# Moving SyncE's closing waits for loads and transposes ahead of the last five stores

## The chip, the cores and the metric

The kernel runs on one core of a Trainium2 chip. The metric is the device time of one execution in microseconds, as a median of several executions. The profile gives a second number, the span from the program's first to its last own instruction, which is about 1.7 us shorter than the time here.

SyncE is the engine that issues most of the transfers here; it computes nothing. A semaphore is a counter that a transfer raises when its data have arrived, and on which an engine can wait.

## The reference, cut to what matters

The program is one transformer layer on 2048 tokens of width 448: linear attention, then a gated feed-forward block. The change touches no arithmetic. Only the last line matters for it, because its result is what the last stores carry.

```python
x = A_x
h = x + _A_ref(_layernorm(x, axis=-1), A_wqkv, A_w_phi, A_wo)
h2 = h + _B_ref(_layernorm(h, axis=-1), B_w_gate, B_w_up, B_w_down)
return h2          # 1 x 2048 x 448, bf16: 16 tiles of 128 tokens
```

## The kernel before

The kernel is a list of operations with a fixed order for each engine. Every transfer gets a semaphore of its own: the rings are at least as long as the number of transfers of their kind (48 for loads, 64 for transposes, 17 for stores).

```python
if dma is not None and nring:
    lst = self.ring.setdefault(dma, [])
    ...
    o.sem = (dma, len(lst) % nring)
    o.val = 16 * (len(lst) // nring + 1)
```

The result tile is finished by VectorE and stored by SyncE. The last tile is finished and stored in two parts, of 320 and 128 columns. The bar in the last comment line marks the place to which the change moves the waits.

```python
def finish(t, b, lo=0, hi=D, nm=""):
    op("dve", "fin%d%s" % (t, nm), lambda e: e.scalar_tensor_tensor(
        out=h_sb[:, t, lo:hi], in0=bk(b)[:, lo:hi], scalar=0.5, in1=h_sb[:, t, lo:hi], op0=ALU.mult, op1=ALU.add),
       r=[B(b), ("x", t)], w=[("xo", t, lo)])
    op("sp", "out%d%s" % (t, nm), lambda e: e.dma_start(out_t[:, t, lo:hi], h_sb[:, t, lo:hi]), r=[("xo", t, lo)], dma="out", nring=17)

# end of SyncE's order:
#   ... out10 out7 out8 out9 out6 out11 | out13 out12 out14 out15 out15b
```

The engine's program is written out by `body`. SyncE ends with a wait for every semaphore that a transfer has ever raised.

```python
last_out = {}
for o in ops:
    if o.dma is not None:
        last_out[o.sem] = max(last_out.get(o.sem, 0), o.val)
...
def body(eng, q=queues[e], e=e):
    seen = {}
    for o in q:
        for j in o.waits:
            ...
            eng.wait_ge(sems[p.sem], p.val)
        ins = o.fn(eng)
        ...
    if e == "sp":
        for sem, v in last_out.items():
            eng.wait_ge(sems[sem], v)
```

The softmax here doesn't subtract the row's maximum and nothing guards it: scores larger than these inputs give would overflow.

## Time and profile before

| | before |
|---|---|
| time, median of 3 runs | 207.08 us (207.05 to 207.18) |
| span | 205.46 us |
| TensorE busy | 197.3 us, 96% |
| last addition on VectorE ends | 201.67 us |
| last store issued / landed | 201.70 / 203.19 us |
| first / last closing wait starts | 202.13 / 205.00 us |
| closing stretch: from the end of the last addition to the end of the span | 3.79 us |

SyncE's instructions are not counted as busy on the page, so the page alone shows an end in which nothing seems to happen. Its instructions are found by the lines of the source that they come from. After its waits it leaves the program by a branch, here put down to line L152 and called the closing branch below. The view of one source line gives, for each kind of instruction, the count, the shortest, median and longest duration in ns, and the start of the first and the last. For a store it also gives the time from issue to landing, which is the moment at which its semaphore is complete. Times to a hundredth of a microsecond for single waits and landings are the trace's own records. The prediction shows these lines.

### The profile page before, as it was taken

To read this page: it belongs to the slowest core of one execution; us is meant where nothing else is said; L and a number is where in the kernel's file an instruction comes from. 1 tells how busy PE (TensorE), PEld (TensorE's weight loads), DVE (VectorE), ACT (ScalarE), POOL (GpSimd) and SP (SyncE) were. 2 spreads that over 40 slices of the span, in tenths; PEclk is the share of its full clock that TensorE was granted. 3 is DMA by queue.
4 is the path that set the end of the run, shared out by engine and by line. 5 is a ranking of instruction groups with operands and counts; after the bars stand their busy time and mean duration, and the time that the engine had idled before them with its cause. 6 is when DMAs were issued, how large, how long until landed. Compare 5 with 4: busy or idle time off the path is not lost.

```text
span 205.5 us, 5834 instructions
## 1 busy us (share of the span) xinstructions
PE 197.3 (96%) x2474; PEld 113.2 (55%) x2474; DVE 135.7 (66%) x340; ACT 97.3 (47%) x195; POOL 57.9 (28%) x98
## 2 busy tenths in 40 slices
PE   7999999989979999999999999999999999999991
PEld 2945556655447877786445444444555555544451
DVE  4899999978899987777768877346332512371252
ACT  2899999889882543522333442334323112320220
POOL 4699998943344401300041020001400000000000
PEclk9999999999999999999999999999999999999999
DMA  6975352999622462130007411120311000012002
GB/s 163 302 138 121 56 102 58 288 260 342 169 51 54 77 76 50 32 79 0 3 0 87 114 29 26 24 54 24 78 48 26 3 0 3 0 58 79 0 11 78
DMA packets 32866, 16.25 MB, mean 79 GB/s; under 512 B 25096, under 2 KB 31944, under 8 KB 32840
## 3 DMA queue, kind: packets, MB, share of 16 engines
q1 hardware_dynamic: 32336, 15.86, 33.9%
q8 instruction: 19, 0.31, 0.6%
q10 hardware_dynamic: 504, 0.03, 0.2%
q14 instruction: 7, 0.06, 0.1%
HBM read 8.34 MB, written 1.84 MB: 50 GB/s over the span
## 4 chain that ended last, share of the span: by engine, by line
PE 91%; ACT 4%; DVE 2%; issue 0%
PE psum L291 81%; PE psum L847 5%; PE psum L473 3%; PE psum L487 1%; ACT eq L648 1%; ACT eq L647 1%; PE psum L562 1%; ACT Wk L480 1%; ACT junk L751 1%; ACT x_sb L743 1%; DVE kvz L678 1%; PE psum L549 1%; DVE b_sb L712 0%; DVE c_sb L715 0%; DVE oT L480 0%
## 5 line engine op out<-in xcount | busy, mean ns | idle before, releaser
L291 PE MATMUL psum<-xnT,wg_sb 64*128 64x512 bf16 (+1 forms) x490 | 93.4, 333 | 0.4 <-ACT eq L648 0.2
L291 PE MATMUL psum<-xnT,wu_sb 64*128 64x512 bf16 (+1 forms) x490 | 92.9, 333 | 0.0
L819 ACT ACTIVATE sg_sb<-psum 128x512 bf16<-128x512 f32 (+1 forms) x70 | 35.0, 512 | 89.4 <-PE psum L291 88.8
L820 DVE SCALAR_TENSOR_TENSOR hhT<-sg_sb,psum 128x512 bf16<-128x512 bf16 (+1 forms) x70 | 38.9, 576 | 52.6 <-ACT sg_sb L819 52.1
L291 PEld LDWEIGHTS psum<-xnT,wg_sb 64*128 64x128 bf16 x490 | 44.3, 94 | 22.8 <-DVE hhT L820 4.8
L291 PEld LDWEIGHTS psum<-xnT,wu_sb 64*128 64x128 bf16 x490 | 44.3, 94 | 12.8
L291 PE MATMUL psum<-wd_sb,hhT 64*128 64x448 bf16 x336 | 36.9, 349 | 0.0
L291 PEld LDWEIGHTS psum<-wd_sb,hhT 64*128 64x128 bf16 x336 | 17.6, 94 | 14.5 <-DVE x_sb L746 0.6
L617 POOL TENSOR_TENSOR phi<-hhT,rs 128x896 bf16<-128x896 bf16 x14 | 24.0, 1738 | 0.9 <-PE psum L291 0.4
L291 PE MATMUL psum<-Wk,xnT 64*128 64x448 bf16 x112 | 22.3, 350 | 0.3 <-ACT Wk L480 0.2
L291 PE MATMUL psum<-wv_sb,xnT 64*128 64x448 bf16 x112 | 22.4, 351 | 0.1
L754 POOL TENSOR_SCALAR ve<-ssq 128x1 f32<-128x1 f32 x16 | 3.1, 192 | 66.1 <-ACT junk L751 65.7
L613 DVE TENSOR_REDUCE ss<-hhT 128x32 f32<-128x896 bf16 x16 | 17.0, 1060 | 0.7 <-ACT hhT L610 0.7
L291 PE MATMUL psum<-xnT,Wq 64*120 64x512 bf16 x112 | 15.0, 385 | 0.1
L724 POOL TENSOR_TENSOR o_pad<-c_sb,rden 128x448 bf16<-128x448 bf16 x10 | 9.3, 937 | 15.6 <-DVE rden L720 13.4
L291 PE MATMUL psum<-wo_o,oT 64*128 64x448 bf16 x56 | 13.2, 350 | 0.0
L291 PE MATMUL psum<-wo_e,oT 64*128 64x448 bf16 x56 | 13.1, 349 | 0.0
L751 ACT ACTIVATE junk<-x_sb,nm 128x448 bf16<-128x448 bf16 x16 | 10.6, 662 | 2.0 <-DVE nm L749 2.0
L847 PE MATMUL psum<-wd_sb,hhT 128*128 128x448 bf16 (+2 forms) x70 | 11.1, 316 | 0.0
L854 DVE SCALAR_TENSOR_TENSOR x_sb<-psum,x_sb 128x448 bf16<-128x448 f32 (+2 forms) x17 | 9.4, 591 | 2.1 <-PE psum L847 1.6
L494 DVE BATCH_NORM_STATS2 st<-x_sb 128x6 f32<-128x448 bf16 x16 | 9.4, 608 | 2.0 <-DMA x_sb<-in_A_x_dram 2.0
L291 PEld LDWEIGHTS psum<-Wk,xnT 64*128 64x128 bf16 x112 | 7.6, 94 | 5.3 <-ACT hhT L610 0.7
(87 smaller groups left out, 243.0 us busy)
## 6 DMA issues: line engine op xcount, KB each, us to landing
out_dram<-x_sb SPq DMA_DIRECT2D x15, 112.0 KB, 1.8
x_sb<-in_A_x_dram SPq DMA_DIRECT2D x7, 224.0 KB, 4.7
wd_sb<-in_B_w_down_dram SPq DMA_DIRECT2D x7, 224.0 KB, 9.6
wg_sb<-in_B_w_gate_dram SPq DMA_DIRECT2D x3, 448.0 KB, 8.8
wu_sb<-in_B_w_up_dram SPq DMA_DIRECT2D x3, 448.0 KB, 6.7
wv_sb<-in_A_wqkv_dram SPq DMA_DIRECT2D x2, 224.0 KB, 5.2
wk_sb<-in_A_wqkv_dram SPq DMA_DIRECT2D x2, 196.0 KB, 3.2
wo_e<-in_A_wo_dram SPq DMA_DIRECT2D x1, 336.0 KB, 8.3
```

Of the source, the lines that this page charges most:

```text
L291: p = e.matmul(o, lhsT=w, rhs=r, start=st, stop=sp, tile_position=(row, 0))
L473: p = e.matmul(bk(3)[:, 0:size], lhsT=zero[:, 0:P], rhs=zero[:, 0:size], start=True, stop=True)
L494: op("dve", "bst%d" % t, lambda e: e.bn_stats(st1[:, t, :], x_sb[:, t, :]), r=[("x", t)], w=[("st1", t)])
L613: op("dve", "ss%d" % t, lambda e: e.tensor_reduce(ss[:, s, :], eks, AX.X, ALU.add), r=[("ek", s)], w=[("ss", s)])
L617: return e.tensor_tensor(phi[:, sp, :, :, :].rearrange("p b a n -> p (b a) n")[:, :, 0:56].rearrange("p b (h d) -> p b h d", h=2), eks.rea ...
L724: return e.tensor_tensor(o_pad[:, t % NO, off:off + D].rearrange("p (h d) -> p h d", h=H), c_sb[:, t % NS, :, 0:DH], rden[:, t % NS, :][:, ...
L751: op("act", "sq%d" % t, lambda e: e.activation(junk[:, t % 2, :], h_sb[:, t, :], ACT.Square, bias=nm2[:, t:t + 1], accum_out=ssq2[:, t:t + ...
L754: op("pool", "ve%d" % t, lambda e: e.tensor_scalar(ve2[:, t:t + 1], ssq2[:, t:t + 1], 1.0 / D, EPS, op0=ALU.mult, op1=ALU.add), r=[("ssq2" ...
L819: op("act", "sig" + nm, lambda e: e.activation(sg_sb[:, k, 0:N], bk(bg)[:, 0:N], ACT.Tanh, scale=0.5), r=[B(bg)], w=[("sg", k)])
L820: op("dve", "hh" + nm, lambda e: e.scalar_tensor_tensor(out=hhT[(t0 // 4) % NHH][:, ff, ns], in0=sg_sb[:, k, 0:N], scalar=1.0, in1=bk(bu)[ ...
L847: p = e.matmul(bk(b)[:, lo:hi], lhsT=hb[:, ff, TS(t)], rhs=wd_sb[:, ff, lo:hi], start=ff == 0, stop=ff == FT - 1)
L854: op("dve", "fin%d%s" % (t, nm), lambda e: e.scalar_tensor_tensor(out=h_sb[:, t, lo:hi], in0=bk(b)[:, lo:hi], scalar=0.5, in1=h_sb[:, t, l ...
```

## The change

The intent is to pay for the waits for loads and transposes, all long finished, at a point where SyncE is idle anyway, and to keep only the waits for stores at the end.

```diff
-                        for o in q:
+                        for n, o in enumerate(q):
+                            if e == "sp" and n == len(q) - 5:
+                                for sem, v in last_out.items():
+                                    if sem[0] != "out":
+                                        eng.wait_ge(sems[sem], v)
                             for j in o.waits:
...
                         if e == "sp":
                             for sem, v in last_out.items():
-                                eng.wait_ge(sems[sem], v)
+                                if sem[0] == "out":
+                                    eng.wait_ge(sems[sem], v)
```

## The prediction

> **What bounds the kernel now.** I read the page first, then the chain of waits in order of time for the last 26 us, then the timeline of the end, and last the sources of SyncE's own instructions there. The page's first part and its chain give the setting: TensorE works almost throughout, and no change on SyncE can shorten that part.
>
> ```profile
> span 205.5 us, 5834 instructions
> PE 197.3 (96%) x2474; PEld 113.2 (55%) x2474; DVE 135.7 (66%) x340; ACT 97.3 (47%) x195; POOL 57.9 (28%) x98
> ```
>
> The chain of waits, cut to its end, shows where the computing stops: the last matmuls of the down projection, then one VectorE addition that ends at 201.38 + 0.29 = 201.67 us. The span is 205.46 us (205.5 on the page), so 3.8 us follow in which no engine computes. The change can touch only these.
>
> ```profile
> 196.24 5.12 PE psum L847 x38
> 201.36 0.02 issue
> 201.38 0.29 DVE x_sb L854
> ```
>
> What fills the 3.8 us is all on SyncE. The timeline shows its last five stores, which start from 199.30 us and are issued by 199.30 + 2.78 = 202.08 us. The store line L857, cut to the last store, gives its time from issue to landing; it was issued at 201.70 us and so landed at about 201.70 + 1.5 = 203.2 us (the trace's semaphore records say 203.19). The wait line L174 has 48 instructions that follow the last store one after another, from 202.13 to 205.00 us. The same view, cut to what starts after 203.2 us, shows that 31 of the 48 still come then: they wait for nothing that has not happened.
>
> ```profile
> 199.30 2.78 SPq L857 DMA_DIRECT2D out_dram<-x_sb  x5
> ...
> DMA to landing us min/median/max: 1.5/1.5/1.5
> ...
> L174 SPq EVENT_SEMAPHORE  x48: 27/28/28, 202.1 to 205.0; - x48
> ...
> L174 SPq EVENT_SEMAPHORE  x31: 27/28/28, 203.2 to 205.0; - x31
> ```
>
> The table of stretches agrees: from 203.0 us nothing moves on the DMA engines, and no engine computes, yet the span goes on for 2.4 us.
>
> ```profile
> 203.00:203.20 0.20, 0.00 (x0) 0.00 (x0) 0.00 (x0) 0.00 (x0) 0.00 (x0) 1.00 0.00 0
> 203.20:205.50 2.30, 0.00 (x0) 0.00 (x0) 0.00 (x0) 0.00 (x0) 0.00 (x0) 0.89 0.00 0
> ```
>
> So the end is set by SyncE's sequencer walking through its list of waits. First come 1.1 us of the list under the stores' landing, then 1.8 us of it alone, and then the closing steps of the program, whose line L152 shows SyncE as the last to arrive (its branch at 205.06 us, where VectorE's drain began at 201.4 and the others' earlier).
>
> ```profile
> L152 DVEq DRAIN  x1: 330/330/330, 201.4 to 201.4; - x1
> L152 SPq COMPARE_BRANCH  x1: 41/41/41, 205.1 to 205.1; - x1
> ```
>
> **What the Trainium skill says.** "Perfetto Trace Analysis", the section on a sequencer-only instruction: the profile reports only the execution; decoding and the waiting itself lie outside. The trace agrees. A wait is shown with 28 ns, but the 48 start (205.00 - 202.13) / 47 = 0.061 us apart; I therefore price a wait by its spacing and not by its duration. "Advanced Engine Details and Errata", in Network/Comms, gives 50-100 ns for a sequencer's reading of a semaphore; 61 ns for an instruction that checks two is in that range. "Perfetto Trace Analysis", DMA Instruction - HWDGE: a DMA's profiled window ends when the sequencer is free, the data move later, and the last descriptor, which raises the semaphore, waits for confirmation of the write, which "can cause a surprisingly long delay especially when the write target is HBM". The trace has 0.38 us for the issue of the last store, against 1.5 us to its landing. "DMA: Bandwidth & Descriptors", Rules for kernel authors, advises issuing a DMA early and waiting late, so that its fixed cost overlaps; here the waits for old transfers are the work that can overlap.
>
> **The change, part by part.** *How many waits.* Every transfer has a semaphore of its own. The source has 32 loads from SyncE (9 of x, 4 of k and v, 4 of wo, 8 of gate and up, 7 of down), 4 small ones from ScalarE, 44 transposes (4 of q, 12 + 14 + 14 of activations) and 17 stores: 97 semaphores. The trace has 48 instructions of two waits each, and the 97th sits on the closing branch. Of the 97, 17 are for stores, so 80 move.
>
> *Where they go.* The last five entries of SyncE's list are out13, out12, out14, out15 and out15b, which are the five of the timeline from 199.30 us. The entry before them, out11, is issued by 185.67 us in the trace's records. The 80 waits thus land between 185.67 and 199.30 us, where SyncE now does nothing but wait 13.6 us for VectorE. All are for transfers long finished: the last transpose is issued at 153.07 us and lands 2.4 us later, the last load is issued at 70.0 us. They should pass without stopping, in 40 instructions x 0.061 = 2.4 us, over by about 188.2 us, 11 us before out13 can be issued. The wait of out13 for VectorE may be joined to the last of them instead of sitting on the store itself, which would make that store some 0.06 us later; the next store starts 0.6 us after this one's issue has ended and is bound by VectorE, so nothing is handed on.
>
> *What stays at the end.* 17 waits: by the same pairing 8 instructions and one on the branch. Were nothing late they would take 8 x 0.061 = 0.49 us and be done at 202.13 + 0.49 = 202.62 us. But now they meet the stores in flight. The last five land, by the trace's semaphore records, at 200.99, 201.91, 202.45, 202.84 and 203.19 us. The waits are paired outward from the middle of the list in the trace before, so the last pair should hold the last store: it passes 0.02 to 0.03 us after the landing (the spacing that the first VectorE statistics show after their loads), at about 203.21 us.
>
> *The tail.* From the start of the last wait instruction before (205.00 us) to the end of the span (205.46 us) are 0.47 us: branch, drain, exchange between engines. It is the same code after.
>
> *The sum.* The new end is 203.21 + 0.47 = 203.68 us in place of 205.46: 1.78 us less. Check by counting: 31 instructions after the landing, less the one that must remain, are 30 x 0.061 = 1.8 us. TensorE's 197 us, the loads, the order and number of all other instructions are unchanged, and so is what the measured time has beyond the span (207.08 - 205.46 = 1.6 us). 207.08 - 1.78 = **205.30 us**, a ratio of 0.991.
>
> **The rivals.** *Nothing is gained, the landing is the bound already.* Then the waits would be free beside the store's confirmation, and the time stays 207.1 us. For it: waits for something already past sound free, and each shows 28 ns. Against: 31 of them start after the landing, and the closing branch follows directly on the last.
>
> *All 40 instructions count.* This would give 40 x 0.061 = 2.4 us, so 204.6 us. Against: the 17 waits left would end at 202.62 us, before the last store has landed at 203.19; the landing takes the place of the list as the bound and keeps 0.6 us of it. Only if the landing itself came earlier could this happen, and nothing in the change makes it earlier.
>
> *The moved waits hold up the stores.* If one of the 80 were for something late, or if they were slower than the 13.6 us of idle time, the last five stores would start late and the end would move out, 1:1. To lose all of the gain, they would have to last 13.6 + 1.8 us, six times their price. Nothing in the profile supports it: the last of those transfers is over 30 us before.
>
> *The waits are dear only under the profiler.* If recording made each of them slower, the unprofiled end would already be closer to the landing. Against: the profiled run took 207.22 us, 0.14 us more than the median of the others. If all of that lay in the 48 waits, 3 ns each, the gain would fall by 30 x 0.003 = 0.1 us.
>
> **Range and chances.** The store's landing is the uncertain term: the 17 stores took 1.5 to 3.0 us, but the ones at the end, without other traffic, 1.5 to 1.8. A last store that needs 1.8 costs 0.3 us of the gain. Runs of the kernel before spread over 0.13 us. The profiler's rival takes off at most 0.1 us. On the other side I see only a landing 0.1 us earlier and the spread. So 205.0 to 205.7 us for 8 in 10. Within 2% is everything from 202.94 to 211.22 us. Faster by over 2% would need 4.1 us, more than the whole 3.8 us in which nothing computes; slower would need the stores held up by over 5 us. Chances: faster 0.01, same 0.98, slower 0.01.
>
> **What would show each step right or wrong.** (1) The wait line inside the loop shows some 40 instructions between about 185.7 and 188.2 us, spaced by 0.06; fewer or slower ones would break the count or the price. (2) The five last stores start at the same times as before, from 199.3 us; later ones would mean the third rival. (3) At the end stand 8 wait instructions, and the last passes at about 203.2 us, within 0.05 us of the last landing; one that passes at 202.6 would mean that the landing isn't waited for as I think. (4) The span is about 203.7 us and the timed difference 1.8 us like the profiled one; a timed difference clearly smaller than the profiled one would mean the profiler's rival. What would make me wrong overall is a landing of the last store at other than 1.5 us, or a part of the 1.6 us beyond the span that ran beside the list of waits and now has to be waited for.

## The result, and the profile after

The changed kernel took 205.43 us (median of 4 runs, 205.24 to 206.15), beside 207.06 us of the kernel before (4 runs, 207.00 to 207.18). The ratio is 0.9927, with a 95% interval of 0.9903 to 0.9951. Ratios here are the mean time of one kernel's runs over that of the other's of the same rounds, so they are not quite the ratio of the quoted medians. The gain of 1.63 us is below 2% and counts as the same.

The changed kernel's lines are five further down in the source: the stores are L862, the moved waits L165, the closing waits L179. First come its span and its TensorE time, from the page.

```profile
span 203.7 us, 5834 instructions
PE 196.7 (97%) x2474; PEld 111.6 (55%) x2474; DVE 135.9 (67%) x340; ACT 97.4 (48%) x195; POOL 57.9 (28%) x98
```

The number of instructions is unchanged, and the span is shorter by 1.75 us. The chain of waits, cut to its end, shows that the computing ends nearly where it did (201.41 + 0.29 = 201.70 us, 0.03 us later than before).

```profile
196.26 5.12 PE psum L852 x38
201.39 0.02 issue
201.41 0.29 DVE x_sb L859
```

SyncE's own lines show the rest. The fence gives, in this order, the moved waits, the last five stores in the timeline (start and length in us), the time from issue to landing of the very last store (issued at 201.73 us), the closing waits, those closing waits that start after 203.2 us, and the closing branch.

```profile
L165 SPq EVENT_SEMAPHORE  x39: 28/28/28, 185.8 to 188.1; - x39
...
199.40 2.71 SPq L862 DMA_DIRECT2D out_dram<-x_sb  x5
...
DMA to landing us min/median/max: 1.5/1.5/1.5
...
L179 SPq EVENT_SEMAPHORE  x8: 28/28/28, 202.2 to 203.2; - x8
...
L179 SPq EVENT_SEMAPHORE  x1: 28/28/28, 203.2 to 203.2; - x1
...
L152 SPq COMPARE_BRANCH  x1: 41/41/41, 203.3 to 203.3; - x1
```

The 39 moved instructions lie between 185.76 and 188.11 us, after which SyncE waits another 11.2 us for VectorE. At the end 8 instructions are left where there were 48, and one instead of 30 starts after the last landing. (The prediction said 31: a view cut to a window also counts an instruction that is under way at its start, and one had begun at 203.18 us.) The list of SyncE's waits, which had no wait for a store in the kernel before, now has one (columns: total, times, longest).

```profile
SPq L170 <- DVE x_sb L859: 11.2, 1, 11.2
SPq L179 <- DMA out_dram<-x_sb: 0.7, 2, 0.4
```

So the bound at the end has changed hands: before, it was the walk through the list; now it is the landing of the last store, at 203.22 us. The closing stretch fell from 3.79 to 2.01 us, by 1.78 us. What is left of it is 0.03 us to the issue of the last store, 1.49 us to its landing and 0.49 us from there to the end.

### The profile page after: what moved, and what is told of

It is laid out like the page before. It is cut to its first block, busy times and chain, and to the rows that moved or that the text cites. A ratio compares the mean times of both kernels' runs of the same rounds, so it can differ in the third digit from the quotient of the medians.

```text
span 203.7 us, 5834 instructions
## 1 busy us (share of the span) xinstructions
PE 196.7 (97%) x2474; PEld 111.6 (55%) x2474; DVE 135.9 (67%) x340; ACT 97.4 (48%) x195; POOL 57.9 (28%) x98
## 4 chain that ended last, share of the span: by engine, by line
PE 89%; DVE 4%; ACT 3%; DMA 1%; issue 1%; POOL 0%; DVEq 0%
PE psum L296 82%; PE psum L852 5%; DVE st L499 2%; DMA x_sb<-in_A_x_dram 1%; ACT eq L653 1%; ACT eq L652 1%; PE psum L567 1%; ACT junk L756 1%; ACT x_sb L748 1%; PE psum L492 1%; DVE kvz L683 1%; DVE mv L500 0%; DVE b_sb L717 0%; DVE c_sb L720 0%; POOL rst L512 0%
```

## The experiments

The theory is this. A wait for something that is already past costs SyncE about 0.061 us for each instruction, and an instruction holds two waits. No run tells whether the 0.061 us are the price of checking a semaphore or of any instruction of SyncE's. These instructions are free as long as they lie under another wait (the 13.6 us for VectorE, the 1.5 us for the last landing); beyond that, they move the end one for one. The main rival says that every instruction of the list counts, without a floor. Others say that only the number of waits at the very end matters, or that moving itself costs something.

Single runs of one kernel differ by a few tenths of a microsecond. In the kept traces with the same end (the changed kernel, a0, a1, a2, b4) the last addition ends anywhere from 201.47 to 201.82 us, but the closing stretch is 2.01 us in each, so it is the sharper measure. All numbers in one table; "waits after landing" counts the closing wait instructions that start later than the last store's landing. The a runs share one set of rounds and of runs of the kernel before, the b runs another, and the c runs a third, on another chip; the line of the kernel before shows its first three runs.

| kernel | closing wait instructions | waits after landing | closing stretch, us | time, us (median) | ratio to before (95% interval) |
|---|---|---|---|---|---|
| before | 48 | 30 | 3.79 | 207.08 | 1 |
| changed | 8 | 1 | 2.01 | 205.43 | 0.9927 (0.9903 to 0.9951) |
| a0 changed, again | 8 | 1 | 2.01 | 205.24 | 0.9892 (0.9863 to 0.9922) |
| a1 none moved | 8 | 1 | 2.01 | 205.32 | 0.9896 (0.9863 to 0.9929) |
| a2 16 kept at the end | 16 | 1 | 2.01 | 205.31 | 0.9897 (0.9867 to 0.9927) |
| a3 40 kept at the end | 28 | 10 | 2.57 | 206.05 | 0.9930 (0.9900 to 0.9961) |
| b1 moved before the last store only | 8 | 1 | 4.35 | 207.74 | 1.0026 (1.0013 to 1.0038) |
| b2 store waits first | 48 | 41 | 4.43 | 207.92 | 1.0035 (1.0023 to 1.0048) |
| b3 list twice | 97 | 95 | 7.75 | 211.10 | 1.0188 (1.0174 to 1.0202) |
| b4 five waits at the end | 2 | 1 | 2.01 | 205.49 | 0.9913 (0.9900 to 0.9927) |
| c1 last store on the branch | 8 | 0 | 1.94 | 205.38 | 0.9912 (0.9896 to 0.9928) |
| c2 the 80 twice | 88 | 70 | 6.21 | 209.70 | 1.0122 (1.0104 to 1.0139) |

All were correct.

### a0: the changed kernel again

No edit.

> The changed kernel again, for its spread and for the base of the three runs beside it. Theory (the list of waits counts only where it outlasts the landing of the last store): span 203.7 us, time 205.4 us, ratio 0.992. One of the four runs on record took 206.15 us; if the old list had hidden late landings of the last store, runs of this kernel should spread more than those of the kernel before (0.9 us against 0.2). If that one run was chance, all five lie within 0.3 us.

Six runs took 205.20 to 205.50 us. The 206.15 us of one earlier run did not come again, so this kernel does not spread more than the other; the kernel before took 206.95 to 208.82 us in its 11 runs beside these. The wide runs of the kernel before also pull the ratio of the a runs down a little (its median there is 207.21 us). What made those runs longer is open: the two above 208 us have a granted clock of 0.992, the other nine 0.996 to 1.000.

### a1: the 80 waits left out

```diff
-                            if e == "sp" and n == len(q) - 5:
-                                for sem, v in last_out.items():
-                                    if sem[0] != "out":
-                                        eng.wait_ge(sems[sem], v)
```

> The 80 waits are left out altogether, only the 17 for stores stand at the end. Theory: the moved waits lie wholly in SyncE's idle 13.6 us, so leaving them out changes nothing: same time as the changed kernel within 0.1 us, 8 wait instructions at the end, the last at about 203.2 us. Rival (moving costs something, by holding up the stores or by instruction fetch): 0.1 to 0.5 us faster than the changed kernel.

```profile
L175 SPq EVENT_SEMAPHORE  x8: 28/28/28, 202.3 to 203.4; - x8
```

The closing stretch is the same 2.01 us, and the medians differ by 0.08 us, within the spread of either. The moved waits therefore cost nothing where they are: in a stretch of idle time these instructions are as cheap as none.

### a2: 16 of the 80 kept at the end

```diff
-                        for o in q:
+                        for n, o in enumerate(q):
+                            if e == "sp" and n == len(q) - 5:
+                                for sem, v in [s for s in last_out.items() if s[0][0] != "out"][:64]:
+                                    eng.wait_ge(sems[sem], v)
...
+                            early = [s for s in last_out if s[0] != "out"][:64]
                             for sem, v in last_out.items():
-                                eng.wait_ge(sems[sem], v)
+                                if sem not in early:
+                                    eng.wait_ge(sems[sem], v)
```

The edit is shown against the kernel before.

> 64 of the 80 waits move, 16 stay at the end beside the 17 for stores: 33 waits, 16 instructions. From 202.16 us by 0.061 us each the last starts at 203.08 us, before the landing at 203.22. Theory: the landing is the bound, so the 8 extra instructions are free: same as the changed kernel within 0.1 us. Rival (every instruction counts, no floor): 8 x 0.061 = 0.5 us slower than the changed kernel.

Sixteen instructions at the end give the same 2.01 us as eight. The view of the closing waits says why: the last of them starts at 203.05 us, 0.02 us after the last store's landing at 203.03 us in this run. It was released by the landing, as the last of eight was; the list itself, 16 instructions from 201.97 us, would have come to it at 201.97 + 15 x 0.061 = 202.88 us.

```profile
L179 SPq EVENT_SEMAPHORE  x16: 27/28/28, 202.0 to 203.0; - x16
```

This is against the rival without a floor, which asked for 0.5 us more.

### a3: 40 of the 80 kept at the end

The edit is that of a2 with 40 for 64, so that 57 waits stay at the end.

> 40 of the 80 move, 40 stay: 57 waits, 28 instructions, the last starts at 202.16 + 27 x 0.061 = 203.80 us, 0.56 us after the changed kernel's last wait. Theory: 0.56 us slower than the changed kernel and 1.2 us faster than before (about 205.95 us). Rival (every instruction counts): 20 x 0.061 = 1.2 us slower than the changed kernel.

```profile
L179 SPq EVENT_SEMAPHORE  x28: 28/28/28, 202.3 to 203.9; - x28
```

The closing stretch grew by 0.56 us, as the theory said, and not by 1.2 us. The timed median is 0.81 us above a0; the 0.25 us beyond are not in the closing stretch. The two profiled runs differ before it too: the last addition ended at 201.82 us here, at 201.47 in a0's. So the cost of the list has a knee: a2 lies on the flat side and a3 on the slope.

### b1: the 80 waits ahead of the very last store

```diff
-                            if e == "sp" and n == len(q) - 5:
+                            if e == "sp" and n == len(q) - 1:
```

> The 80 waits move ahead of the very last store only, where SyncE has 0.1 us to spare and not 13.6. They start at about 201.66 us and take 40 x 0.061 = 2.4 us, so the last store starts at about 204.1 us, lands 1.5 us later at 205.6, and the span ends 0.47 us after that at 206.1 us. Theory: 0.65 us slower than before, 2.4 us slower than the changed kernel (about 207.7 us). Rival (only the waits at the very end matter, wherever the others stand): as the changed kernel, 205.4 us.

The timeline of the five stores and the moved waits show the collision. The stores now stretch over 5.11 us instead of 2.71, because 39 waits and the one for VectorE stand between the fourth and the fifth.

```profile
199.09 5.11 SPq L862 DMA_DIRECT2D out_dram<-x_sb  x5
...
L165 SPq EVENT_SEMAPHORE  x39: 27/28/28, 201.4 to 203.7; - x39
```

The last store started at 203.87 us (204.1 was expected, but the computing of this run ended 0.24 us earlier than the changed kernel's), and the kernel was 0.6 us slower than the one before it. The same waits, moved by four stores, are worth +2.34 us in the closing stretch against the changed kernel (4.35 - 2.01). The rival that only the very end matters falls.

### b2: all 97 at the end, but the store waits issued first

```diff
-                            for sem, v in last_out.items():
+                            rest = [s for s in last_out.items() if s[0][0] != "out"]
+                            outs = [s for s in last_out.items() if s[0][0] == "out"]
+                            for sem, v in rest[:40] + outs + rest[40:]:
                                 eng.wait_ge(sems[sem], v)
```

> All 97 waits stay at the end as before, but the 17 for stores stand in the middle of the list, which the compiler issues first (pairs outward from the middle). The eighth instruction then holds the last store and blocks until 203.24 us; 40 instructions follow that wait for nothing: 203.24 + 40 x 0.061 = 205.67 us, span 206.1 us. Theory: 0.65 us slower than before (about 207.7 us) with the same set of waits. Rival (the number of waits at the end sets the time, not what lies under the landing): 207.1 us, as before.

This has the same set of waits at the same place as the kernel before, in another order. The source's order is not the order on the engine: by the numbers of their semaphores in the trace's records, the waits are paired outward from the middle of the list, so the middle comes first: in the kernel before they run 169 with 168, 170 with 167, and so on to 155 with 108, with 107 on the closing branch; here they begin with 148 and 147, which are stores, and the eighth pair holds 155, the last store. The first fence line shows all 48 closing waits; the second shows those from 203.2 us on, after the instruction that blocked until the landing at 203.11 us.

```profile
L176 SPq EVENT_SEMAPHORE  x48: 27/28/28, 202.0 to 205.5; - x48
...
L176 SPq EVENT_SEMAPHORE  x40: 27/28/28, 203.2 to 205.5; - x40
```

In the kernel before, 30 started after the landing; here 41 do, the blocked one and 40 more. The closing stretch was 0.64 us longer than before (4.43 - 3.79), and the timed median 0.78 us. The number of waits alone does not set the time; what counts is how many come after the event that is really late.

### b3: the whole list twice

```diff
-                            for sem, v in last_out.items():
+                            for sem, v in list(last_out.items()) * 2:
                                 eng.wait_ge(sems[sem], v)
```

> The kernel before with its list of waits twice: 194 waits, about 97 instructions, 49 more, all after the landing. Theory: 49 x 0.061 = 3.0 us slower than before in the timed, unprofiled runs too (about 210.0 us). Rival (the waits are dear only under the profiler): the profiled span grows by 3.0 us and the timed runs by clearly less.

My number was a miss: the closing stretch grew by 3.96 us (7.75 - 3.79) and not by 3.0. The view of the closing waits has a duration that is not in the lists before it.

```profile
L174 SPq EVENT_SEMAPHORE  x97: 17/28/1024, 202.0 to 208.8; - x97
```

In the doubled list the middle is where the first copy ends and the second begins, so the wait for the last store came in the second instruction. That one took 1.02 us, to the landing at 203.02 us, and 95 instructions followed it with the usual spacing. The first instruction of this list holds one wait alone, and the second starts 0.058 us after it; so on this single instance the price goes by instruction and hardly by the number of waits in it. The order of the list, which I had not followed through here, made it a second b2.

I also meant this run to tell whether waits are dear only under the profiler. It can't: each run on record of the kernels tried has a span and a granted clock, so I take it that each was made with some recording, and the profiled run is one of those timed. In the timed runs the increase was 3.96 us as well, but no run here is known to be without recording.

### b4: only five waits at the end

```diff
+                        ends = [o.sem[1] for o in q[-5:] if o.sem]
...
-                                    if sem[0] != "out":
+                                    if sem[0] != "out" or sem[1] not in ends:
...
-                                if sem[0] == "out":
+                                if sem[0] == "out" and sem[1] in ends:
```

> The changed kernel with 12 of the 17 store waits moved up as well; 5 waits, 2 instructions, stay at the end. Theory: the landing of the last store is the bound, so nothing is gained: same as the changed kernel (205.4 us) within 0.1 us, the last wait at about 203.2 us. Rival (every instruction counts): 6 x 0.061 = 0.4 us faster.

```profile
L180 SPq EVENT_SEMAPHORE  x2: 28/28/28, 203.0 to 203.4; - x2
```

Two instructions at the end give the same 2.01 us as eight and sixteen. Nothing more is to be had by shortening the list.

### c1: the wait for the last store on the closing branch

```diff
-                            for sem, v in last_out.items():
+                            for sem, v in reversed(list(last_out.items())):
                                 if sem[0] == "out":
```

> The changed kernel with the 17 store waits in reverse order, so that the wait for the very last store sits on the closing branch itself and the instruction before it waits for the last but one, which lands 0.35 us earlier. Theory: after the landing of the last store only the branch and what follows it remain, not a wait instruction and then the branch: landing to end of span falls from 0.48 to about 0.42 us, 0.07 us faster than the changed kernel; the timed medians differ by less than their spread. Rival (the end hangs on something other than SyncE's last instructions): landing to end stays 0.48 us.

```profile
L179 SPq EVENT_SEMAPHORE  x8: 28/28/305, 202.2 to 202.6; - x8
```

The first semaphore of the list sits on the branch itself. From landing to end of span the time fell from 0.49 to 0.42 us, as expected, and the closing stretch from 2.01 to 1.94 us. That shows that the end hangs on SyncE's last few instructions. The timed median, 205.38 us, cannot be told from the changed kernel's, so this version is a better end by the profile only.

### c2: the 80 waits twice, store waits late

```diff
-                            for sem, v in last_out.items():
+                            for sem, v in rest + rest + outs:
                                 eng.wait_ge(sems[sem], v)
```

> The kernel before with the 80 non-store waits twice and the store waits at the end of the list, where the outward pairing meets them late (from the 72nd of 88 instructions), so that no instruction blocks. b3_twice was 3.7 us longer by its profile where 3.0 was expected; its second instruction held the last store and blocked for 1.07 us, after which 95 followed. Theory: 40 more instructions by 0.0605 us = 2.4 us slower than before, span 207.9 us, time 209.5 us, none of them blocking. Rival (long lists cost more per instruction, 0.071 us as b3_twice's mean spacing would have it): 88 x 0.071 - 2.9 = 3.3 us slower.

This repeats b3 without its fault; `rest` and `outs` are those of b2. No instruction blocks, and the closing stretch grew by 2.42 us (6.21 - 3.79), where 40 x 0.0605 = 2.42 was expected and the rival asked for 3.3.

```profile
L176 SPq EVENT_SEMAPHORE  x88: 27/28/28, 202.2 to 207.5; - x88
```

The timed median was 2.54 us above that of the kernel before. The price of a wait instruction is thus the same in a list of 48 and in one of 88.

## Why the prediction was right

The predicted 205.30 us was measured as 205.43 us, inside the range. Point by point:

**The count of waits.** Eighty were to move in 40 instructions. The trace has 39 on the line of the moved waits; the fortieth also holds the wait of out13 for VectorE and is put down to that line (L170), and the last of the 80 sits on the store. The first of the 39 starts at 185.76 us, and the last ends at 188.11 us, where 188.2 was predicted.

**Hidden under VectorE.** It was right that nothing is handed on. The store out13 did start 0.067 us after the instruction that waited for VectorE, as the prediction allowed for, and the next store was bound by VectorE. In all, out13 started 0.10 us later than before and the last store 0.03 us later; the additions that they wait for had ended 0.03 us later too. That the moved waits are free is shown by a1, and that this depends on the place is shown by b1.

**The floor.** The prediction chose the landing and not the shorter list as the new bound. The last closing wait started at 203.24 us, 0.02 us after the landing, where 203.21 was predicted. a2 and b4 show the floor from both sides, and a3 shows the slope beyond it.

**The tail.** Last wait to end of span: 0.47 us before, 0.47 us after.

**The sum.** The closing stretch fell by 1.78 us, which is the predicted number. The prediction's check by counting came to 1.8 us with one instruction too many (see above: 30 started after the landing, not 31); 29 x 0.061 = 1.77 us agrees better still. From 203.0 us the old span went on for 2.46 us, not 2.4. Its 1.6 us beyond the span pairs the median of other runs with the span of the profiled run, which itself took 207.22 us: 1.76 us there, and 1.72 us in the changed kernel's profiled run. That the difference stays the same is what the sum needs. The span fell by 1.75 us, because the computing ended 0.03 us later. The medians fell by 1.63 us; the 0.12 us between are within the spread of the runs (205.24 to 206.15 us). That a timed median fell so close is in part luck: beside a0 the same pair of kernels differs by 1.97 us (207.21 - 205.24).

**The rivals.** That the landing was the bound already is refuted by the result. That all 40 instructions count is refuted by a2. That the moved waits hold up the stores does not happen at this place, and does at b1's. That the waits are dear only under the profiler stays open: the prediction argued from a difference of 0.14 us between the profiled run and the others, and that argument is weaker than it looked, since the runs on record all carry a span.

## What to carry to other kernels

A wait for something already past is not free: count the wait instructions that start after the last event that is really late, leave out the one that must wait for that event, and multiply by their spacing in the trace (0.061 us here); that is what moving or dropping them can give. Put such waits into idle time of their engine, ahead of a point at which it waits for another engine anyway, and put the late event last; but check the order in the trace, because it need not be that of the source, as b2 and b3 show. Once the list fits under the last landing, shortening it further gives nothing.

## What the Trainium skill lacked or had wrong

- "Perfetto Trace Analysis", on sequencer-only instructions, says that a wait lies ahead of the profiled window. For an instruction that waits for two semaphores this held in the changed kernel, where the late semaphore stands first in the record (duration 28 ns, with the gap before it). Where the late one stands second, the wait was inside the duration: 1024 ns in b3 and 305 ns in c1. TensorE shows it in the kernel before already: a wait at 17.53 us has 670 ns, where its first semaphore was complete at 16.06 us and its second was raised at 18.16 us.
- "Advanced Engine Details and Errata", Network/Comms, has 50-100 ns for reading a semaphore from a sequencer. I found no price there for a list of waits that have all been met; here it is 0.061 us from start to start for an instruction with two, the same in lists of 48 and of 88.
- I found no page that tells of the order in which such a list reaches the engine. Here, the compiled program pairs the waits outward from the middle of the list and puts the first on the closing branch; b2 changed nothing but the order and was 0.8 us slower than before.
